# Sliding-window attention and a gated feed-forward block: where the attention ends, a fifth block by seven products, and sums on GpSimd

## The chip, the cores and the metric

The kernel runs on one core of one Trainium2 chip. A core has TensorE (PE, matrix products), VectorE (DVE) and ScalarE (ACT), which take TensorE's results out of PSUM, GpSimd (POOL), which can't reach PSUM and here issues the loads, and SyncE (SP), which issues stores and transposing transfers. The metric is the device time of one execution in microseconds, the median of several runs. A profile is of one execution of its own.

## The reference

```
attention, for each of 8 batches and 8 heads, 576 rows of 64:
scores = q k^T / 8, minus slope_h * distance, only where 0 <= distance < 128
attn = softmax(scores) v
x = attn as 4608 rows of 512 (8 heads of 64 side by side)
g = x w_gate          (512 -> 1536)
h = silu(g) * (x w_val)
out = h w_out         (1536 -> 512), float32
```

## The kernel before

**Attention.** The 4608 rows are cut into 36 tiles of 128, counted i = 0 to 35: two batches give nine tiles, the ninth of which joins the two last 64 rows. For each tile there are loads of q, k and v (from the POOL queue, seven tiles ahead, `loads_to`), transposed copies of q and k (`kT` has 12 places, `qT` 9), score products, an Exp on ScalarE, a multiplication with a mask on VectorE (lines 303 and 335), the products with v (line 359), a reciprocal and a multiplication (lines 362 and 363), and a transfer that writes the tile transposed into `xT` (line 381).

**Feed-forward.** Nine blocks n of 512 rows; block 8 collects the joined tiles, so it needs the last tile. A block has 12 slices m of 128 hidden columns. *Directly*, a slice is a product pg with the gate weights and one pv with the value weights, four matmuls of 512 columns each (line 415). pg and pv turn through three PSUM buffers. The gate is x*sigmoid(x), here made of Tanh on ScalarE (line 433), which shares its table with Exp, one VectorE instruction on pg (uu, line 434) and one on pv (hT, line 445); hT is twice the value, and the projection halves it.

*By seven products* (Strassen's scheme in Winograd's form), two slices make a unit u: seven products of four matmuls of 256 columns (line 639) stand for eight. They need sums of the weights (`gate_val_weight_sums`, four subtractions a unit of 128x512 f16) and of x (`x_sums`, four a block). Their gate is ScalarE's Silu, which needs another table, so it can only begin when the last Exp is done. `SEVEN_FROM = 6`: blocks 6, 7 and 8 go so.

**Projection.** From block 1 on the second product goes by seven products too (`strassen`, line 550): 14 parts a block of six matmuls of 256 columns, interleaved with the next block's first products. They need sums of h (`sums`, lines 503 to 506, in three chunks c of four instructions), which are put into a list, `later`, and issued one or two a step.

**Order.** The feed-forward generator yields steps: 1.0 for a direct product, 0.75 for a part of the projection, 0.5 for a product by seven. `everything` advances the attention to a target: from step 60 on, 84 + (step - 57) * RATE / 34.5 attention steps (line 1016); a direct block has 34.5 steps. TensorE's order is then as written; DVE and ACT are ordered by the scheduler, which may run an instruction earlier than it is written; POOL's and SP's queues keep the written order. In block 5, behind slice `SILU_AT = 7`, `attention_ends` runs what is left of the attention and brings in the Silu table (line 979); slices 8 to 11 then use Silu directly (lines 431 and 442). The weight sums and the sums of x go into `later` on VectorE (lines 613 to 616). Their results lie in places of kT, qT and the masks that the attention no longer needs (`t_homes`, `spare`).

Of the kernel before, what the change touches and what calls it, by code (L numbers as in the profile page):

```python
# [11 lines left out]
FP16 = mybir.dt.float16  # L12
# [17 lines left out]
FIRST = 4  # L30
LEAD = 6
PRE = 0
SEVEN_FROM = 6
SILU_AT = 7
SECOND = 5.5
RATE = 54.0
FIXED_FROM = 60
LATE = 13


def slot(h):
# [11 lines left out]
def kernel(  # L53
# [366 lines left out]
        return ps  # L420

    acted = {}
    by_silu = set()

    def gate(n, m, pg, c0=0, c1=512):

        if (n, m) not in acted:
            acted[(n, m)] = [supool.tile([P, 512], FP16, name=i, tag=i) for i in ("tt", "uu")]
        tt, uu = (t_[:, c0:c1] for t_ in acted[(n, m)])
        if (n, m) in by_silu:  # L430
            nc.scalar.activation(tt, pg[:, c0:c1], AF.Silu)
            return
        nc.scalar.activation(tt, pg[:, c0:c1], AF.Tanh, scale=0.5)  # L433
        nc.vector.scalar_tensor_tensor(out=uu, in0=tt, scalar=one if (n, m) == PIN else 1.0,  # L434
                                       in1=pg[:, c0:c1], op0=ALU.add, op1=ALU.mult)

    def val(n, m, pv, c0=0, c1=512):

        if n not in hT:
            hT[n] = hpool.tile([P, NMB, 512], FP16, name="hT", tag="hT")  # L440
        if (n, m) in by_silu:
            nc.vector.scalar_tensor_tensor(out=hT[n][:, m, c0:c1], in0=acted[(n, m)][0][:, c0:c1], scalar=2.0,
                                           in1=pv[:, c0:c1], op0=ALU.mult, op1=ALU.mult)
            return
        nc.vector.tensor_mul(hT[n][:, m, c0:c1], acted[(n, m)][1][:, c0:c1], pv[:, c0:c1])  # L445
# [52 lines left out]
    one_more = []  # L498
    hsum = {}

    def four_sums(a11, a12, a21, a22, s2, s3, s4):

        return [lambda: nc.vector.tensor_sub(s3, a11, a21),
                lambda: nc.vector.tensor_add(a21, a21, a22),
                lambda: nc.vector.tensor_sub(s2, a21, a11),
                lambda: nc.vector.tensor_sub(s4, a12, s2)]

    def at_once(fs):
        for f in fs:
            f()  # L510

    def sums(n, c):
# [7 lines left out]
        return four_sums(a11, a12, a21, a22, s2, s3, s4)  # L520

    def strassen(n, t):

# [3 lines left out]
        S2, S3, S4 = hsum[n]  # L527
        cols = slice(t * P, (t + 1) * P)
        end = n == NBLK - 1
        seeded = SEVEN_FROM <= n + 1 < NBLK  # L530
        factor = 1.0 if n >= SEVEN_FROM else 0.5
        if end:
            X, Y = (ps_a.tile([P, HC], FP32, name="po", tag="a", bufs=4) for _ in range(2))
# [73 lines left out]
    t_homes = [halves(kT[:, n]) for n in range(NK)] + [halves(qT[:, n]) for n in range(NQ)] + spare[6:9]  # L607

    def gate_val_weight_sums(u):

        cols = slice(2 * u * P, (2 * u + 2) * P)
        t1, t2, t3, t4 = tsum[u] = t_homes[4 * u:4 * u + 4]
        return [lambda: nc.vector.tensor_sub(t1, V1[:, :, cols], G1[:, :, cols]),
                lambda: nc.vector.tensor_sub(t3, V2[:, :, cols], V1[:, :, cols]),
                lambda: nc.vector.tensor_sub(t2, V2[:, :, cols], t1),
                lambda: nc.vector.tensor_sub(t4, G2[:, :, cols], t2)]

    def x_sums(n):

        a11, a12 = xT[n][:, 0:HK, 0:256], xT[n][:, HK:NKB, 0:256]  # L620
        a21, a22 = xT[n][:, 0:HK, 256:512], xT[n][:, HK:NKB, 256:512]
        s2, s3, s4 = xsum[n] = spare[3 * (n % 2):3 * (n % 2) + 3]
        return four_sums(a11, a12, a21, a22, s2, s3, s4)

    later = []

    def gate_val_by_seven(n):

        x = xT[n]
        A11, A12 = x[:, 0:HK, 0:256], x[:, HK:NKB, 0:256]  # L630
        S1, A22 = x[:, 0:HK, 256:512], x[:, HK:NKB, 256:512]
        S2, S3, S4 = xsum.pop(n)
        hT[n] = hpool.tile([P, NMB, 512], FP16, name="hT", tag="hT")
        live = {}

        def product(dst, w, c0, a, start=False):
# [59 lines left out]

    def seven_steps():

        units = [(n, u) for n in range(SEVEN_FROM, NBLK) for u in range(NMB // 2)]
        of = {}  # L700
        for i, (n, u) in enumerate(units):
            if u == 0:
                of[n] = gate_val_by_seven(n)
            now, before = (n, u), units[i - 1] if i else None
            if i + 1 < len(units):
                turn = (("first", now), ("seventh", before), ("fifth", now), ("sixth", now),
                        ("fourth", before), ("second", now), ("third", now))
            else:
                turn = (("first", now), ("seventh", before), ("fifth", now), ("sixth", now),
                        ("fourth", before), ("second", now), ("seventh", now), ("third", now),  # L710
                        ("fourth", now))
            for k, (name, which) in enumerate(turn):
                if which is not None:
                    of[which[0]][name](which[1])
                yield n, 7 * u + k, name, which
# [3 lines left out]
    def ffn():  # L719

        for n in range(NBLK):
            if n > 1:
                parts = chain(strassen(n - 1, 0), strassen(n - 1, 1))
            if n == 1:
                begin(2, 2, 1)
                begin(3, 3, 1)
                for j in range(PRE):
                    for _ in project(0, j, ps_f, "po", 1):
                        yield 1.0
            if n == SEVEN_FROM:  # L730
                break
            due, given = 0, 0
            for m in range(NMB):
                for half, _ in enumerate(gate_val(n, m)):
                    scored[0] = False
                    yield 1.0
                    due += n > 1 and 2 * m + half in AT
                    while due and not (scored[0] and given % 7 == 1):
                        next(parts)
                        due, given = due - 1, given + 1  # L740
                        yield 0.75
                    if n > 1:
                        for _ in range(1 + (len(later) > 3)):
                            if later:
                                later.pop(0)()
                if n == 1:
                    if m in (4, 6, 8, 10):
                        for _ in project(0, m // 2 - 2, ps_f, "po", 1):
                            yield 1.0
                    if m in (4, 6, 8):  # L750
                        weight_sums(m // 2 - 2)
                if n > 0 and m >= 9:
                    (at_once if n == 1 and m < 11 else later.extend)(sums(n, m - 9))
                if n + 1 == SEVEN_FROM:
                    if m == SILU_AT:
                        attention_ends()
                        by_silu.update((n, i) for i in range(m + 1, NMB))
                    if m in (SILU_AT + 1, SILU_AT + 2):
                        later.extend(gate_val_weight_sums(m - SILU_AT - 1))
                    if m == SILU_AT:  # L760
                        later.extend(x_sums(n + 1))
            if n > 1:
                assert next(parts, 0) == 0
        ends = [strassen(NBLK - 1, t) for t in range(2)]
        tail = ExitStack()
        for n, k, name, which in seven_steps():
            if k == 0 and n > SEVEN_FROM:
                assert next(parts, 0) == 0
                parts = chain(strassen(n - 1, 0), strassen(n - 1, 1))
            if n == SEVEN_FROM and k in (1, 3, 10, 17):  # L770
                later.extend(gate_val_weight_sums(2 + (k + 4) // 7))
            yield 0.5
            if k % 3 == 2 and k < 42:
                next(parts)
                yield 0.75
            if k == 20 and n + 1 < NBLK:
                later.extend(x_sums(n + 1))
# [97 lines left out]
    def attention():  # L875
# [5 lines left out]
        for i in range(FIRST, last + 1):  # L881
# [10 lines left out]
            if not late or i == last:  # L892
                weighted(i)
                yield i
            loads_to(i + 7)
            ahead(i)
            yield i - len(waiting)
            if late and i < X_DMA_FROM:
# [155 lines left out]
```

## Time and profile before

| what | us |
|---|---|
| median of 3 runs | 334.12 (333.97 to 334.51) |
| the profiled execution: time | 334.78 |
| the profiled execution: span | 333.0 |
| TensorE busy | 324.5 |
| VectorE busy | 273.4 |
| ScalarE busy | 202.5 |
| GpSimd busy (issuing loads) | 111.1 |
| last v products of the attention begin | 222 |
| first product by seven (line 639) begins | 236.61 |

The time is some 1.8 us longer than the span, which counts from the program's first to its last instruction. The page's slices are 8.3 us each, and a digit is the busy share in tenths. The ends of matmuls are modelled, so the cost of a product is better read from one start to the next. In the timeline, the first two numbers of a line are start and length in us, and `x4` counts the instructions merged into it.

### The profile page before, as it was taken

What the parts mean: (1) busy time and instruction counts of PE and PEld (TensorE: products, weight loads), DVE (VectorE), ACT (ScalarE), POOL (GpSimd) and SP (SyncE); (2) the same over time, 40 slices, a digit from 0 to 9 for tenths busy, and PEclk for the clock granted to TensorE, in tenths of its full rate; (3) what the DMA queues carried; (4) which work ended last, traced back from release to release, by engine and by line L of the source; (5) the groups of instructions that cost most, each with busy time, mean ns of one, the idle gap of its engine ahead of it and who ended that gap; (6) DMA issues with size and microseconds to landing.
All of it is one profiled execution on the core that took longest, in us unless ns stands there. A gap on an engine that the chain in (4) does not pass through costs nothing.

```text
span 333.0 us, 7659 instructions
## 1 busy us (share of the span) xinstructions
PE 324.5 (97%) x2919; PEld 216.6 (65%) x2919; DVE 273.4 (82%) x643; ACT 202.5 (61%) x404; POOL 111.1 (33%) x138
## 2 busy tenths in 40 slices
PE   8999999999999999999999999999999999999994
PEld 4575465544455655556555665666788888888884
DVE  3579878999798889987999999999854985775683
ACT  4885777465665656457456365563567666776650
POOL 8977776468853254553535000000000000000000
PEclk9999999999999999999999999999999999999999
DMA  9999999999999999999999664231100101011014
GB/s 151 171 182 175 174 186 166 119 131 182 178 173 142 189 159 150 165 151 185 197 132 164 136 81 111 18 94 19 65 31 33 63 2 66 25 42 63 2 63 128
DMA packets 166565, 38.82 MB, mean 117 GB/s; under 512 B 154368, under 2 KB 162176, under 8 KB 166528
## 3 DMA queue, kind: packets, MB, share of 16 engines
q0 software_dynamic: 118880, 18.62, 80.9%
q1 hardware_dynamic: 46960, 19.08, 30.5%
q10 hardware_dynamic: 688, 0.62, 0.6%
q8 instruction: 23, 0.38, 0.5%
q14 instruction: 14, 0.11, 0.1%
HBM read 37.91 MB, written 9.44 MB: 142 GB/s over the span
## 4 chain that ended last, share of the span: by engine, by line
PE 85%; DVE 10%; ACT 2%; issue 1%; DVEq 0%
PE po L550 18%; PE pg L415 16%; PE pv L415 15%; PE gX L639 9%; PE gY L639 5%; PE av L359 5%; PE ps L291 3%; PE p L550 3%; DVE uu L434 2%; PE gZ L639 2%; DVE hT L445 2%; PE psc L327 2%; PE po L469 2%; DVE ex L303 1%; ACT tt L433 1%
## 5 line engine op out<-in xcount | busy, mean ns | idle before, releaser
L415 PE MATMUL pv<-xT,wv_sb 128*128 128x512 f16 (+2 forms) x312 | 76.6, 363 | 0.3 <-DVE uu L434 0.2
L415 PE MATMUL pg<-xT,wg_sb 128*128 128x512 f16 (+2 forms) x324 | 76.5, 355 | 0.1
L433 ACT ACTIVATE tt<-pg 128x512 f16<-128x512 f32 x68 | 40.9, 603 | 48.9 <-PE pg L415 48.9
L297 ACT ACTIVATE ex<-ps 128x512 f16<-128x512 f32 x96 | 50.1, 607 | 8.0 <-PE ps L291 8.0
L434 DVE SCALAR_TENSOR_TENSOR uu<-tt,pg 128x512 f16<-128x512 f16 x67 | 45.6, 680 | 7.7 <-ACT tt L433 7.4
L190 POOL DMA_DIRECT2D kn<-in_k_dram x39 | 33.2, 854 | 43.9 <-DMA kT<-kn 31.4
L445 DVE TENSOR_TENSOR hT<-uu,pv 128x512 f16<-128x512 f16 x68 | 46.1, 679 | 1.6
L415 PEld LDWEIGHTS <-wg_sb 128*128 128x128 f16 x324 | 28.7, 98 | 24.0 <-issue 2.2
L550 PEld LDWEIGHTS <-hT 128*128 128x128 f16 x384 | 37.1, 98 | 10.7 <-issue 0.8
L415 PEld LDWEIGHTS <-wv_sb 128*128 128x128 f16 x312 | 27.9, 98 | 24.8 <-issue 2.3
L184 POOL DMA_DIRECT2D va<-in_v_dram x40 | 34.4, 866 | 15.5 <-DMA kT<-kn 6.6
L190 POOL DMA_DIRECT2D qn<-in_q_dram x39 | 33.3, 863 | 8.7 <-DMA qT<-qn 3.2
L550 PEld LDWEIGHTS <-S 128*128 128x128 f16 x288 | 27.5, 98 | 8.0 <-issue 1.5
L303 DVE TENSOR_TENSOR ex<-ex,m_reg 128x1024 f16<-128x1024 f16 x42 | 28.5, 684 | 2.8 <-ACT ex L297 2.8
L363 DVE TENSOR_TENSOR x<-av,rec 128x256 f16<-128x256 f32 x72 | 28.4, 419 | 0.5
L550 PE MATMUL po<-T,S 128*128 128x256 f16 x192 | 25.9, 273 | 0.3 <-ACT u2s L576 0.3
L550 PE MATMUL po<-T,hT 128*128 128x256 f16 x192 | 26.0, 273 | 0.0
L331 ACT ACTIVATE exc<-psc 128x512 f16<-128x512 f32 x40 | 21.4, 608 | 3.2 <-PE psc L327 3.1
L693 DVE TENSOR_TENSOR hT<-s,v 128x512 f16<-128x512 f16 x18 | 7.6, 424 | 17.7 <-ACT s L692 17.7
L359 PEld LDWEIGHTS <-ex 128*128 128x128 f16 x384 | 17.5, 98 | 4.4 <-issue 1.0
L359 PE MATMUL av<-va,ex 128*128 128x65 f16 x384 | 19.3, 193 | 0.3 <-ACT ex L297 0.3
L291 PE MATMUL ps<-qT,kT 64*128 64x256 f16 x192 | 15.9, 272 | 1.4 <-DVE qT L222 0.6
(129 smaller groups left out, 522.3 us busy)
## 6 DMA issues: line engine op xcount, KB each, us to landing
out_dram<-osb SPq DMA_DIRECT2D x32, 256.0 KB, 2.2
va<-in_v_dram POOLq DMA_DIRECT2D x32, 128.0 KB, 6.2
qn<-in_q_dram POOLq DMA_DIRECT2D x31, 128.0 KB, 6.6
kn<-in_k_dram POOLq DMA_DIRECT2D x31, 128.0 KB, 6.2
wg_sb<-in_moe_w_gate_dram POOLq DMA_DIRECT2D x6, 256.0 KB, 7.6
wo_sb<-in_moe_w_out_dram POOLq DMA_DIRECT2D x3, 512.0 KB, 8.4
wv_sb<-in_moe_w_val_dram POOLq DMA_DIRECT2D x5, 256.0 KB, 7.6
kn<-in_k_dram POOLq DMA_DIRECT2D x8, 64.0 KB, 4.7
```

The source lines that it names most:

```text
L184: nc.gpsimd.dma_start(va[rank][p0:p1, :, 0:D], src)
L190: nc.gpsimd.dma_start(t_[p0:p1], src)
L297: nc.scalar.activation(e[:, o:o + 2, :], banks[q4][par], AF.Exp, scale=scale)
L303: nc.vector.tensor_mul(e[:, o, :], e[:, o, :], reg[:, o, :])
L359: nc.tensor.matmul(av[:, j, :], w, val, start=(n == 0), stop=(n == len(todo) - 1))
L363: nc.vector.tensor_mul(x[:, 4 * half:4 * half + 4, :], av[:, :, 0:D], rec.broadcast_to([P, 4, D]))
L415: nc.tensor.matmul(ps[:, c0:c1], w[:, kb, ms], xT[n][:, kb, c0:c1], start=(kb == 0 and c0 == 0), stop=(kb == NKB - 1 and c1 == 512), skip_ ...
L433: nc.scalar.activation(tt, pg[:, c0:c1], AF.Tanh, scale=0.5)
L434: nc.vector.scalar_tensor_tensor(out=uu, in0=tt, scalar=one if (n, m) == PIN else 1.0, in1=pg[:, c0:c1], op0=ALU.add, op1=ALU.mult)
L445: nc.vector.tensor_mul(hT[n][:, m, c0:c1], acted[(n, m)][1][:, c0:c1], pv[:, c0:c1])
L550: nc.tensor.matmul(dst, a[:, m, cols], b[:, m, :], start=(start and m == 0), stop=(m == HM - 1), skip_group_check=True)
L639: nc.tensor.matmul(dst[:, i, :], w[:, kb, c0 + i * P:c0 + (i + 1) * P], a[:, kb, :], start=(start and i == 0 and kb == 0), stop=(i == 1 an ...
```

## The change

- Block 5 goes by seven products from slice 4 on (`SEVEN_FROM = 5`, `UNIT_FROM = 2`: its units 2 to 5). Slices 0 to 3 stay direct, with Tanh; their hT is halved on the spot (the factor 0.5 in line 438's function), since a block by seven holds h itself. The direct Silu slices are gone.
- `attention_ends` stands behind slice 3 of block 5, and RATE is 59.
- All weight sums run on GpSimd: those of the first three units used (u = 2, 3, 4) are issued at attention tiles 29, 30 and 33, the other three behind the attention's end. The sums of x of block 5 run on GpSimd at tile 31, with a place of their own for s1, as the direct slices still read x. The first chunk of the h sums of blocks 3 and 4 runs on GpSimd, behind slice 10.
- The places of all these sums are chosen anew, by when the attention frees them. In `strassen` the second product of block 4's first half keeps its old buffers, and block 4's projection runs on among the units of block 5.

```diff
-SEVEN_FROM = 6
-SILU_AT = 7
+SEVEN_FROM = 5
+UNIT_FROM = 2
 SECOND = 5.5
-RATE = 54.0
+RATE = 59.0
...
+SUMS_BY_POOL = {3, 4}
...
-        if (n, m) in by_silu:
-            nc.vector.scalar_tensor_tensor(out=hT[n][:, m, c0:c1], in0=acted[(n, m)][0][:, c0:c1], scalar=2.0,
+        if n == SEVEN_FROM:
+            nc.vector.scalar_tensor_tensor(out=hT[n][:, m, c0:c1], in0=acted[(n, m)][1][:, c0:c1], scalar=0.5,
                                            in1=pv[:, c0:c1], op0=ALU.mult, op1=ALU.mult)
...
-        seeded = SEVEN_FROM <= n + 1 < NBLK
+        seeded = SEVEN_FROM <= n + 1 < NBLK and (n >= SEVEN_FROM or t > 0 or UNIT_FROM == 0)
...
+    turns = [(UNIT_FROM + n) % (NMB // 2) for n in range(NMB // 2)]
+    t_homes = dict(zip(turns, (early_homes[0:4], early_homes[4:8], early_homes[12:16],
+                               late_homes[0:4], late_homes[4:8], late_homes[8:12])))
...
-        return [lambda: nc.vector.tensor_sub(t1, V1[:, :, cols], G1[:, :, cols]),
-                lambda: nc.vector.tensor_sub(t3, V2[:, :, cols], V1[:, :, cols]),
-                lambda: nc.vector.tensor_sub(t2, V2[:, :, cols], t1),
-                lambda: nc.vector.tensor_sub(t4, G2[:, :, cols], t2)]
+        t1, t2, t3, t4 = tsum[u] = t_homes[u]
+        return [lambda: nc.gpsimd.tensor_sub(t1, V1[:, :, cols], G1[:, :, cols]),
+                lambda: nc.gpsimd.tensor_sub(t3, V2[:, :, cols], V1[:, :, cols]),
+                lambda: nc.gpsimd.tensor_sub(t2, V2[:, :, cols], t1),
+                lambda: nc.gpsimd.tensor_sub(t4, G2[:, :, cols], t2)]
...
-            for m in range(NMB):
+            for m in range(2 * UNIT_FROM if n == SEVEN_FROM else NMB):
...
-                if n > 0 and m >= 9:
+                if n > 0 and m >= 9 and (m > 9 or n not in SUMS_BY_POOL):
                     (at_once if n == 1 and m < 11 else later.extend)(sums(n, m - 9))
...
+                if m == 10 and n in SUMS_BY_POOL:
+                    at_once(sums(n, 0, nc.gpsimd))
+            if n == SEVEN_FROM:
+                break
...
+        attention_ends()
+        for u in turns[3:]:
+            at_once(gate_val_weight_sums(u))
...
+            if i in (29, 30):
+                at_once(gate_val_weight_sums(turns[i - 29]))
+            if i == 31:
+                at_once(x_sums(SEVEN_FROM))
+            if i == 33:
+                at_once(gate_val_weight_sums(turns[2]))
```

More of the change, by code (lines that the diff above doesn't have):

```diff
@@ L422 @@
     acted = {}
-    by_silu = set()
     def gate(n, m, pg, c0=0, c1=512):
@@ L429, in gate @@
         tt, uu = (t_[:, c0:c1] for t_ in acted[(n, m)])
-        if (n, m) in by_silu:
-            nc.scalar.activation(tt, pg[:, c0:c1], AF.Silu)
-            return
         nc.scalar.activation(tt, pg[:, c0:c1], AF.Tanh, scale=0.5)
@@ L440, in val @@
             hT[n] = hpool.tile([P, NMB, 512], FP16, name="hT", tag="hT")
-        if (n, m) in by_silu:
-            nc.vector.scalar_tensor_tensor(out=hT[n][:, m, c0:c1], in0=acted[(n, m)][0][:, c0:c1], scalar=2.0,
+        if n == SEVEN_FROM:
+            nc.vector.scalar_tensor_tensor(out=hT[n][:, m, c0:c1], in0=acted[(n, m)][1][:, c0:c1], scalar=0.5,
                                            in1=pv[:, c0:c1], op0=ALU.mult, op1=ALU.mult)
@@ L499, with four_sums @@
     hsum = {}
[L501 to L506, printed above, removed]
+    def four_sums(a11, a12, a21, a22, s2, s3, s4, s1=None, eng=nc.vector):
+        s1 = a21 if s1 is None else s1
+        return [lambda: eng.tensor_sub(s3, a11, a21),
+                lambda: eng.tensor_add(s1, a21, a22),
+                lambda: eng.tensor_sub(s2, s1, a11),
+                lambda: eng.tensor_sub(s4, a12, s2)]
     def at_once(fs):
@@ L510, in at_once, with sums @@
             f()
-    def sums(n, c):
+    def sums(n, c, eng=nc.vector):
         if n not in hsum:
@@ L519, in sums @@
         s2, s3, s4 = (t_[:, lo, :] for t_ in hsum[n])
-        return four_sums(a11, a12, a21, a22, s2, s3, s4)
+        return four_sums(a11, a12, a21, a22, s2, s3, s4, eng=eng)
     def strassen(n, t):
@@ L606 @@
     spare += [halves(m_[:, 4 * n:4 * n + 4, :]) for m_ in msk for n in range(2)]
-    t_homes = [halves(kT[:, n]) for n in range(NK)] + [halves(qT[:, n]) for n in range(NQ)] + spare[6:9]
+    early_homes = [halves(t_[:, n]) for t_, n in ((kT, 0), (kT, 1), (kT, 2), (kT, 3), (qT, 0), (kT, 4),
+                                                  (qT, 1), (kT, 5), (qT, 2), (qT, 3), (kT, 7), (qT, 4),
+                                                  (kT, 8), (qT, 5), (kT, 9), (qT, 6))]
+    late_homes = [halves(t_[:, n]) for t_, n in ((kT, 6), (kT, 10), (kT, 11), (qT, 7), (qT, 8))] + spare[3:10]
+    turns = [(UNIT_FROM + n) % (NMB // 2) for n in range(NMB // 2)]
+    t_homes = dict(zip(turns, (early_homes[0:4], early_homes[4:8], early_homes[12:16],
+                               late_homes[0:4], late_homes[4:8], late_homes[8:12])))
+    x_homes = {SEVEN_FROM: early_homes[8:11] + early_homes[11:12]}
+    for n in range(SEVEN_FROM + 1, NBLK):
+        x_homes[n] = early_homes[8:11] if (n - SEVEN_FROM) % 2 == 0 else spare[0:3]
     def gate_val_weight_sums(u):
         cols = slice(2 * u * P, (2 * u + 2) * P)
-        t1, t2, t3, t4 = tsum[u] = t_homes[4 * u:4 * u + 4]
-        return [lambda: nc.vector.tensor_sub(t1, V1[:, :, cols], G1[:, :, cols]),
-                lambda: nc.vector.tensor_sub(t3, V2[:, :, cols], V1[:, :, cols]),
-                lambda: nc.vector.tensor_sub(t2, V2[:, :, cols], t1),
-                lambda: nc.vector.tensor_sub(t4, G2[:, :, cols], t2)]
+        t1, t2, t3, t4 = tsum[u] = t_homes[u]
[3 more added lines that the diff above has]
+                lambda: nc.gpsimd.tensor_sub(t4, G2[:, :, cols], t2)]
     def x_sums(n):
@@ L621, in x_sums @@
         a21, a22 = xT[n][:, 0:HK, 256:512], xT[n][:, HK:NKB, 256:512]
-        s2, s3, s4 = xsum[n] = spare[3 * (n % 2):3 * (n % 2) + 3]
-        return four_sums(a11, a12, a21, a22, s2, s3, s4)
+        s2, s3, s4 = x_homes[n][0:3]
+        s1 = x_homes[n][3] if n == SEVEN_FROM else a21
+        xsum[n] = s1, s2, s3, s4
+        return four_sums(a11, a12, a21, a22, s2, s3, s4, s1, nc.gpsimd if n == SEVEN_FROM else nc.vector)
     later = []
@@ L630, in gate_val_by_seven @@
         A11, A12 = x[:, 0:HK, 0:256], x[:, HK:NKB, 0:256]
-        S1, A22 = x[:, 0:HK, 256:512], x[:, HK:NKB, 256:512]
-        S2, S3, S4 = xsum.pop(n)
-        hT[n] = hpool.tile([P, NMB, 512], FP16, name="hT", tag="hT")
+        A22 = x[:, HK:NKB, 256:512]
+        S1, S2, S3, S4 = xsum.pop(n)
+        if n not in hT:
+            hT[n] = hpool.tile([P, NMB, 512], FP16, name="hT", tag="hT")
         live = {}
@@ L697, in seven_steps @@
     def seven_steps():
-        units = [(n, u) for n in range(SEVEN_FROM, NBLK) for u in range(NMB // 2)]
+        units = [(n, u) for n in range(SEVEN_FROM, NBLK)
+                 for u in range(UNIT_FROM if n == SEVEN_FROM else 0, NMB // 2)]
         of = {}
         for i, (n, u) in enumerate(units):
-            if u == 0:
+            if n not in of:
                 of[n] = gate_val_by_seven(n)
@@ L729, in ffn @@
                         yield 1.0
-            if n == SEVEN_FROM:
+            due, given = 0, 0
+            if n == SEVEN_FROM and not UNIT_FROM:
                 break
-            due, given = 0, 0
-            for m in range(NMB):
+            for m in range(2 * UNIT_FROM if n == SEVEN_FROM else NMB):
                 for half, _ in enumerate(gate_val(n, m)):
@@ L751, in ffn @@
                         weight_sums(m // 2 - 2)
-                if n > 0 and m >= 9:
+                if n > 0 and m >= 9 and (m > 9 or n not in SUMS_BY_POOL):
                     (at_once if n == 1 and m < 11 else later.extend)(sums(n, m - 9))
[L754 to L761, printed above, removed]
+                if m == 10 and n in SUMS_BY_POOL:
+                    at_once(sums(n, 0, nc.gpsimd))
+            if n == SEVEN_FROM:
+                break
             if n > 1:
                 assert next(parts, 0) == 0
+        attention_ends()
+        for u in turns[3:]:
+            at_once(gate_val_weight_sums(u))
         ends = [strassen(NBLK - 1, t) for t in range(2)]
@@ L769, in ffn @@
                 parts = chain(strassen(n - 1, 0), strassen(n - 1, 1))
-            if n == SEVEN_FROM and k in (1, 3, 10, 17):
-                later.extend(gate_val_weight_sums(2 + (k + 4) // 7))
             yield 0.5
-            if k % 3 == 2 and k < 42:
-                next(parts)
+            if k % 3 == 2 and k < 42 and next(parts, 1) is None:
                 yield 0.75
```

## The prediction

> **What bounds the kernel now.** I read the page from the top: busy shares first, then the slices, then the chain of waits, then sums of busy time by stage.
>
> ```profile
> PE 324.5 (97%) x2919; PEld 216.6 (65%) x2919; DVE 273.4 (82%) x643; ACT 202.5 (61%) x404; POOL 111.1 (33%) x138
> ...
> PE   8999999999999999999999999999999999999994
> ...
> DVE  3579878999798889987999999999854985775683
> ...
> POOL 8977776468853254553535000000000000000000
> ...
> PE 85%; DVE 10%; ACT 2%; issue 1%; DVEq 0%
> ```
>
> TensorE is busy nearly everywhere and carries 85% of the chain that ended last. VectorE is the only other engine with a share there. It stands at 9 in slices 18 to 26, which is the last third of the attention. GpSimd does nothing after slice 21. The sums by stage (us, then busy PE, PEld, DVE, ACT, POOL) sharpen this:
>
> ```profile
> 150.00:190.00 40.00, 39.93 (x374) 24.20 (x373) 38.15 (x92) 23.03 (x47) 15.13 (x19) 1.00 1.70 165
> 190.00:222.00 32.00, 32.00 (x298) 19.12 (x297) 31.58 (x79) 19.64 (x40) 0.00 (x0) 1.00 0.40 71
> 222.00:236.60 14.60, 14.56 (x103) 8.75 (x100) 14.53 (x40) 5.02 (x11) 0.00 (x0) 1.00 0.23 55
> 236.60:264.10 27.50, 27.50 (x253) 24.65 (x252) 18.05 (x40) 19.00 (x38) 0.00 (x0) 1.00 0.10 40
> ```
>
> From 190 to 222 us both TensorE and VectorE have no idle time. From 236.6 us on, the blocks by seven products, VectorE is free a third of the time. So there are two questions: how many TensorE microseconds go, and what happens to a VectorE that has nothing to spare. How near it stands to TensorE's need is seen in the timeline around the end of the attention (start, length, engine):
>
> ```profile
> 218.20 1.02 PE L415 MATMUL pg<-xT,wg_sb 128*128 128x512 f16 x4
> 219.06 1.03 PE L415 MATMUL pv<-xT,wv_sb 128*128 128x512 f16 x4
> 220.74 1.03 PE L415 MATMUL pg<-xT,wg_sb 128*128 128x512 f16 x4
> 221.43 0.68 DVE L434 SCALAR_TENSOR_TENSOR uu<-tt,pg 128x512 f16<-128x512 f16 x1
> 222.33 1.02 PE L415 MATMUL pv<-xT,wv_sb 128*128 128x512 f16 x4
> ```
>
> pg and pv turn through three PSUM buffers, so the pv at 222.33 takes the buffer of the pg at 218.20. VectorE frees that at 221.43 + 0.68 = 222.11, which is 0.22 us before TensorE wants it.
>
> **TensorE: the products.** From the same lines a direct product (four matmuls of 512 columns) costs 219.06 - 218.20 = 0.86 us from start to start. Two slices m are four products, 3.45 us. A unit by seven does the same work in seven products of four matmuls of 256 columns:
>
> ```profile
> 241.63 0.60 PE L639 MATMUL gY<-xT,kT 128*128 128x256 f16 x4
> 242.06 0.60 PE L639 MATMUL gX<-m_reg,kT 128*128 128x256 f16 x4
> 242.50 0.60 PE L639 MATMUL gX<-xT,kT 128*128 128x256 f16 x4
> 242.94 0.82 PE L550 MATMUL po<-T,S 128*128 128x256 f16 x6
> ```
>
> That is (242.94 - 241.63)/3 = 0.437 us each, 3.06 us a unit. A unit saves 0.39 us. Slices 4 to 11 of block 5 become four units: 4 x 0.39 = **1.6 us less**, all of it on the path, since TensorE sets it. Nothing else on TensorE changes in number: the second projection's products and the attention are the same matmuls, elsewhere.
>
> **ScalarE.** Eight activations (8 x 0.60) become four units of two Silu and three copies (20 x 0.59): 7.0 us more within about 18 us. The full blocks by seven already run so, with ScalarE at 19.0 of 27.5 us and TensorE without idle time, so this is hidden at 0. The table load (1.28 us at 219.88) now comes just ahead of the first unit, not four slices ahead of it. At present TensorE does not stop over it. The first unit's sixth product waits for a ScalarE copy of the first; if that copy stands behind the load, I bound the wait by 0 and 1.28 us and take 0.3, since a fifth product (0.44) and a part of the projection (0.65) lie between.
>
> **VectorE: what goes.** Its instructions overlap at the ends: the timeline steps 0.60 us behind one of 0.68 and 0.33 behind one of 0.41. The 24 weight sums are 24 x 0.33 = 8 us, and they are not run behind the attention, where the program puts most of them: 14 of the 24 start before 222 us (lines 613 to 616, from 150.1 us on), and 3 sums of x too. In 190 to 222 that is 4 + 3 sums, 2.3 us. Four h sums of block 4 go as well, 1.3 us. Against it the attention is pressed together: 283 attention steps end at step 57 + (283-84) x 34.5/54 = 184 of the ffn count now, and at 57 + (283-84) x 34.5/59 = 173 with RATE 59. Block 5 begins at 163.5 and its four direct slices end at 175, so nothing is left over to be run in a heap. Per ffn step the attention rises by 9%, TensorE's time by some 2%: VectorE's attention work in this stretch (masks 6.8, x and rec 6.2 us) grows by about 0.8 us. Sum: 0.4 idle + 2.3 + 1.3 - 0.8 = **3.2 us of air in 32**. By itself this buys no time, since the waits of 190 to 222 us name none of TensorE; earlier, in the five 20 us windows from 60 to 160 us, TensorE's busy time lacks 1.2 us in all. I bound the gain by 0 and that 1.2 us and take 0.2.
>
> **GpSimd: what comes.** 24 weight sums, 4 sums of x, 8 of h: 36 instructions on two SBUF inputs of 128x512 f16. The trace has none on this engine. From below one costs what VectorE needs, 0.33 us; from above the longest instruction of any compute engine but TensorE, the 1.28 us table load. I take 0.87, GpSimd's only row of work (issuing a load, 0.85 to 0.87 us). All loads are issued by 181 us, so only the h sums of block 3 have loads behind them (rank 33 on); in the trace that rank's v load waits until 171.76 us anyway. Behind that, twelve sums are queued at tiles 29 to 31; tile 29 comes at step 143, block 4's h sums at 158, and a step takes about 1 us (a block's 34.5 steps span 36 us), so they have 15 us: at 0.87 they take 10.4, at 1.28 15.4. The h sums are due at the third part of the next projection, 9 steps after their place. So GpSimd's own lateness costs 0 at either end.
>
> The open price is what GpSimd does to VectorE. Before the first unit 20 of these instructions run in about 32 us. From below each costs VectorE nothing; from above each holds it for its whole length, 20 x 0.87 = 17 us. VectorE's instructions with two SBUF inputs in 190 to 222 (masks, h sums, fillers) are about a third of its busy time, so I take a third of half the length, 20 x 0.14 = 2.9 us, just inside the 3.2 us of air: cost 0.3 us.
>
> The Trainium skill ("SBUF — State Buffer", section "Who interferes with whom") speaks against this change: a VectorE instruction with two SBUF inputs contends with a GpSimd one that reads SBUF, and the later one waits for the whole of the other. The trace shows no such pair. The skill's "GPSIMD Engine Reference", section 3.1, gives about 2.6 cycles of 1.2 GHz an element for two inputs, an estimate of 1.1 us here; by these two pages some 15 of the 20 would hold VectorE for half of that, 8 us, and the sum would be about 2.5 us slower instead of faster.
>
> **Sum.** -1.6 + 0.3 (switch) - 0.2 + 0.3 = **-1.2 us**. The span of 333.0 becomes 331.8. The profiled execution took 334.78, 0.66 above the median of the runs, so I put the difference on the median: 334.12 - 1.2 = **332.9 us**.
>
> **Rivals.**
> 1. *VectorE held by GpSimd* (slower). Place: tiles 29 to 35, before the first unit. Each of 20 GpSimd sums meets a mask or an h sum and holds it for half its length: 20 x 0.44 = 8.7 us, less 3.2 us of air and about 1 us of buffers, 4.5 us of TensorE waiting for PSUM: 334.1 - 1.6 + 4.5 = 337.0. It decides from a hold of 0.25 us per instruction on ((3.2 + 1.6)/20). For it: 0.22 us between uu and pv. Against it: two thirds of VectorE's time is on PSUM or single inputs, and its air is real. A half-sized hold gives 335.
> 2. *GpSimd late* (slower): at 2.0 us an instruction the twelve take 24 us, block 4's h sums start 9 us late, and the first two of them end 13 us after their place against 9: 4 us of stop, 332.9 + 4 = 336.9. It decides from 1.7 us an instruction (12 x 1.7 - 15 + 2 x 1.7 = 8.8).
> 3. *Given back*: the 1.6 us goes to the switch of tables and to attention latencies, since the masks and AV of a tile have 9% less other work between them (TensorE's busy time falls to 19.44 of 20 us between 120 and 140 us, beside masks): within 0.2%, 333.5 to 334.8.
> 4. *Air pays*: an unfilled VectorE ends earlier before each AV, and the 1.2 us that TensorE lacks between 60 and 160 us goes: 332.9 - 1.2 = 331.7.
>
> **How the numbers follow.** Forecast 0.45 (332.2 to 333.4), rival 4 0.08, rival 3 0.13, rival 1 0.27, rival 2 0.07. Faster by over 0.2% (0.67 us, about what a measurement here can tell from no change): 0.53. Same: 0.13. Slower: 0.34. The range runs from just under rival 4's 331.7 to just past rival 1's 337.0, and leaves out the far end of the holding price and a gain above 2.5 us.
>
> **What would show it.** Right: the four units of block 5 at 0.437 us a product; the first unit (L639) starting near 217 us, 20 us sooner than now (the fifth direct slice now begins at 214.67, and some 2 us of TensorE's attention work behind it moves ahead); VectorE below 95% in the 32 us ahead of it; no weight sums on it. Wrong: masks, h sums or products of two SBUF inputs on VectorE that last longer than 0.68 and 0.42 us while GpSimd works, pv matmuls waiting for uu, L550 waiting for a GpSimd sum, or a GpSimd sum above 1.3 us.

## The result and the profile after

The changed kernel takes **347.52 us** (median of 4 runs, 345.02 to 348.12) beside 334.19 us before. The ratio is 1.038 with an interval of 1.0355 to 1.0413: 13 us slower, where 1.2 us faster was forecast. The profiled execution took 347.09 us, its span 345.3. Times are medians, and the two executions that ran in a slower state (663.12 us in run 1, 351.50 us in run 11) are left out of them.

First the page of the changed kernel: busy times, four rows of the 40 slices, and the shares of the chain of waits.

```profile
PE 325.5 (94%) x2967; PEld 221.8 (64%) x2967; DVE 277.9 (80%) x615; ACT 209.4 (61%) x416; POOL 156.2 (45%) x174
...
PE   8999999999999999999988994979999999999994
...
DVE  4778978999797799888998989885885785785582
...
POOL 8977774639835274366849766690000000000000
PEclk9999999999999999999999998799999999999999
...
PE 63%; DVE 20%; DMA 8%; issue 4%; ACT 3%; ACTq 0%; DVEq 0%
```

TensorE's share of the chain fell from 85 to 63%, VectorE's doubled from 10 to 20%, and DMA, which had none, has 8%. TensorE's row has a hole at slice 25, and just there the granted clock, which stood at 9 in every slice before, drops. From block 6 on nothing differs: 96.4 us to the end of the span in both (236.6 to 333.0 before, 248.9 to 345.3 after). Block 4 starts 2.0 us later than before, block 5 6.2 us, and block 6 12.3 us. So most of the loss lies in blocks 4 and 5, where 32 of the 36 GpSimd sums run.

The sums by stage (start:end, us, then busy PE, PEld, DVE, ACT, POOL, the granted TensorE clock as a share of full speed, DMA share, GB/s), first of the kernel before:

```profile
200.00:210.00 10.00, 10.00 (x86) 5.84 (x86) 10.00 (x28) 5.38 (x12) 0.00 (x0) 1.00 0.34 93
210.00:220.00 10.00, 10.00 (x101) 6.03 (x102) 10.00 (x24) 6.27 (x14) 0.00 (x0) 1.00 0.26 28
```

then of the changed kernel, around the hole:

```profile
200.00:210.00 10.00, 9.25 (x92) 5.52 (x91) 9.39 (x16) 5.79 (x12) 8.67 (x7) 1.00 0.04 9
210.00:220.00 10.00, 5.81 (x31) 2.72 (x31) 9.13 (x16) 2.45 (x5) 4.50 (x5) 0.66 0.37 86
220.00:230.00 10.00, 8.70 (x88) 5.79 (x87) 10.00 (x20) 4.39 (x8) 9.84 (x9) 1.00 0.13 26
```

In the changed kernel VectorE is busy for 9.13 to 10 of every 10 us, but with 16 to 20 instructions, where 24 to 28 filled such a 10 us before. A busy share that stays while the count falls means longer instructions. VectorE's timeline in front of the hole (start, length):

```profile
207.77 1.64 DVE L336 TENSOR_TENSOR exc<-exc,m_reg 128x1024 f16<-128x1024 f16 x1
209.33 1.37 DVE L503 TENSOR_TENSOR S<-hT 128x512 f16<-128x512 f16 x1
210.62 1.37 DVE L501 TENSOR_TENSOR S<-hT 128x512 f16<-128x512 f16 x1
211.91 1.63 DVE L336 TENSOR_TENSOR exc<-exc,m_c 128x1024 f16<-128x1024 f16 x1
213.46 0.67 DVE L431 SCALAR_TENSOR_TENSOR uu<-tt,pg 128x512 f16<-128x512 f16 x1
```

and GpSimd's, for the same stretch:

```profile
206.23 1.34 POOL L620 TENSOR_TENSOR kT<-wv_sb,wg_sb 128x512 f16<-128x512 f16 x1
207.53 1.33 POOL L621 TENSOR_TENSOR kT<-wv_sb 128x512 f16<-128x512 f16 x1
208.82 1.59 POOL L622 TENSOR_TENSOR qT<-wv_sb,kT 128x512 f16<-128x512 f16 x1
210.49 1.21 POOL L623 TENSOR_TENSOR qT<-wg_sb,qT 128x512 f16<-128x512 f16 x1
211.66 1.33 POOL L620 TENSOR_TENSOR kT<-wv_sb,wg_sb 128x512 f16<-128x512 f16 x1
```

Laid side by side they take strict turns. GpSimd's sum ends at 207.53 + 1.33 = 208.86, and the mask ends 0.55 us later, at 209.41. GpSimd's next sum is listed from 208.82, but it ends 1.00 us after that mask, at 210.41; VectorE's sum ends 0.29 us behind it. By these ends it looks as if neither engine worked while the other did. The four VectorE instructions take 5.7 us from start to start (207.77 to 213.46); by the steps that the prediction read (0.60 a mask, 0.33 a sum) they need 1.9. The `uu` at 213.46 was queued behind them, and it frees the PSUM buffer of a `pg`. TensorE's timeline:

```profile
208.23 1.03 PE L416 MATMUL pg<-xT,wg_sb 128*128 128x512 f16 x4
214.19 1.87 PE L416 MATMUL pv<-xT,wv_sb 128*128 128x512 f16 x4 [4.93 <-DVE uu L431]
215.85 1.49 PE L548 MATMUL po<-wo_sb,hT 128*128 128x256 f16 x6
217.27 1.04 PE L328 MATMUL psc<-qT,kT 64*128 64x128 f16 x16
218.23 1.72 PE L416 MATMUL pg<-xT,wg_sb 128*128 128x512 f16 x4
219.79 1.03 PE L416 MATMUL pv<-xT,wv_sb 128*128 128x512 f16 x4
```

The stop of 4.93 us is the hole. The four groups behind it run at about half rate: 1.66, 1.42, 0.96 and 1.56 us from start to start, where undisturbed ones take 0.86, 0.65, 0.55 and 0.86. That is 2.7 us more. The clock in the row of 210 to 220 us is 0.66 because it is half of full speed for part of it:

```profile
212.80:219.60 6.80, 5.41 (x30) 2.59 (x30) 5.93 (x14) 2.08 (x5) 1.38 (x3) 0.50 0.27 51
```

VectorE's groups over the whole kernel, by shape (count, then busy us and mean ns), the changed kernel's first:

```profile
L304 DVE TENSOR_TENSOR ex<-ex,m_reg 128x1024 f16<-128x1024 f16 x42 | 31.1, 747 | 4.6 <-ACT ex L298 4.4
L501 DVE TENSOR_TENSOR S<-hT 128x512 f16<-128x512 f16 x22 | 11.8, 545 | 0.0
L336 DVE TENSOR_TENSOR exc<-exc,m_c 128x1024 f16<-128x1024 f16 x12 | 10.5, 879 | 4.5 <-ACT exc L332 4.3
L336 DVE TENSOR_TENSOR exc<-exc,m_reg 128x1024 f16<-128x1024 f16 x7 | 7.5, 1073 | 1.8 <-ACT exc L332 1.8
```

and one of the kernel before:

```profile
L303 DVE TENSOR_TENSOR ex<-ex,m_reg 128x1024 f16<-128x1024 f16 x42 | 28.5, 684 | 2.8 <-ACT ex L297 2.8
```

Before, every mask group had a mean of 683 to 686 ns and every group of h sums 414 to 418. Only instructions that read two SBUF tiles (masks, sums of h and of x) grew; `uu` and `hT`, which read PSUM, kept 0.68 us. Counted one by one, 19 VectorE instructions were lengthened, by 13.9 us together (0.73 each). GpSimd's 36 sums take 46.0 us, mean 1.28; those that meet nothing take 1.15.

**A ledger on TensorE** of the two profiled executions. New waits: pv for uu 5.7 - 0.2 = 5.5; the output projection for `osb` (VectorE's copy out of PSUM) 2.3; scores for q's transposing transfer 1.5 + 1.1 = 2.6. Half clock 2.7. Units -1.6. Sum +11.5, of 347.09 - 334.78 = 12.3. The rest is not assigned.

### The profile page after: what moved, and what is told of

The parts are those of the page before. It is cut to its first block, busy times and chain, and to the rows that moved or that the text cites. A ratio compares the mean times of both kernels' runs of the same rounds, so it can differ in the third digit from the quotient of the medians.

```text
span 345.3 us, 7787 instructions
## 1 busy us (share of the span) xinstructions
PE 325.5 (94%) x2967; PEld 221.8 (64%) x2967; DVE 277.9 (80%) x615; ACT 209.4 (61%) x416; POOL 156.2 (45%) x174
## 4 chain that ended last, share of the span: by engine, by line
PE 63%; DVE 20%; DMA 8%; issue 4%; ACT 3%; ACTq 0%; DVEq 0%
PE po L548 14%; PE gX L649 11%; PE pv L416 9%; PE pg L416 8%; DMA qT<-qn 7%; PE gY L649 5%; DVE uu L431 4%; DVE hT L442 3%; PE gZ L649 3%; PE av L360 3%; PE p L548 2%; DVE exc L336 2%; DVE ex L304 2%; PE ps L292 2%; DVE x L364 2%
## 5 line engine op out<-in xcount | busy, mean ns | idle before, releaser
L416 PE MATMUL pv<-xT,wv_sb 128*128 128x512 f16 (+2 forms) x280 | 69.2, 365 | 5.9 <-DVE uu L431 5.7
L416 PE MATMUL pg<-xT,wg_sb 128*128 128x512 f16 (+3 forms) x292 | 69.0, 356 | 0.5 <-DVE hT L442 0.4
L430 ACT ACTIVATE tt<-pg 128x512 f16<-128x512 f32 x64 | 38.6, 604 | 41.9 <-PE pg L416 41.8
L431 DVE SCALAR_TENSOR_TENSOR uu<-tt,pg 128x512 f16<-128x512 f16 x63 | 42.8, 680 | 6.9 <-ACT tt L430 6.6
L416 PEld LDWEIGHTS <-wv_sb 128*128 128x128 f16 x280 | 25.1, 98 | 29.2 <-issue 10.4
L442 DVE TENSOR_TENSOR hT<-uu,pv 128x512 f16<-128x512 f16 x60 | 40.7, 680 | 1.8 <-PE pv L416 0.3
L416 PEld LDWEIGHTS <-wg_sb 128*128 128x128 f16 x292 | 25.7, 98 | 22.5 <-issue 3.2
L304 DVE TENSOR_TENSOR ex<-ex,m_reg 128x1024 f16<-128x1024 f16 x42 | 31.1, 747 | 4.6 <-ACT ex L298 4.4
L703 DVE TENSOR_TENSOR hT<-s,v 128x512 f16<-128x512 f16 x22 | 9.3, 425 | 19.8 <-ACT s L702 19.8
L664 ACT COPY p<-gY 128x512 f32<-128x512 f32 x22 | 12.9, 585 | 12.2 <-PE gY L649 11.8
```

Source lines behind the costliest of these rows:

```text
L304: nc.vector.tensor_mul(e[:, o, :], e[:, o, :], reg[:, o, :])
L416: nc.tensor.matmul(ps[:, c0:c1], w[:, kb, ms], xT[n][:, kb, c0:c1], start=(kb == 0 and c0 == 0), stop=(kb == NKB - 1 and c1 == 512), skip_ ...
```

## The experiments

Theory 1: GpSimd's sums hold VectorE because both read SBUF, each instruction waiting for the other's whole length. Theory 2: the units, the denser attention or the table switch cost the time. Theory 3, formed on the way: the pressed attention also outruns its transfers.

**1. All 36 sums back on VectorE** (everything else as in the changed kernel).

```
-        return [lambda: nc.gpsimd.tensor_sub(t1, ...
+        return [lambda: nc.vector.tensor_sub(t1, ...
...
-                    at_once(sums(n, 0, nc.gpsimd))
+                    at_once(sums(n, 0))
```

> The changed kernel with all 36 sums back on VectorE, everything else as changed. Theory 1 (GpSimd's sums hold VectorE's two-input instructions): masks back at 0.68 us and sums at 0.42, the 5 us stop of TensorE at 209 us gone; VectorE has some 12 us of sums more, so 333 to 337 us. Theory 2 (the attention is pressed too hard, whoever makes the sums): still 344 us or more, since VectorE gets more to do.

Measured 336.9 us (six executions, 335.67 to 338.08), ratio 1.007 (1.004 to 1.0099). No lengthened instruction: masks 0.685. 10.6 of the 13.3 us are gone, as theory 1 said, at the upper end of its range. 2.7 us above the kernel before are left, so something else costs too (runs 3, 6 and 8).

**2. Only the weight sums of the kernel before on GpSimd** (24 sums, no other edit: `nc.vector` to `nc.gpsimd` in the same four lines).

> The kernel before with its 24 weight sums on GpSimd, nothing else. Theory 1: masks and h sums beside them are held by up to 1 us each, 24 GpSimd sums of 1.2 us; VectorE loses 8 us of its own sums and gains up to 15 us of holding: 335 to 341 us. Theory 2: 333 to 334.5 us, as VectorE is relieved.

342.40 us, ratio 1.0244 (1.0208 to 1.028). With no unit, no RATE and no switch touched, 24 sums (31.5 us on GpSimd) cost 8.2 us; 13 VectorE instructions are lengthened, by 8.4. pv waits 2.7 us for uu. The cost exceeds what was expected, as did that of the change.

**3. Only RATE 54 to 59 in the kernel before.**

> The kernel before with RATE 59 alone: the attention runs 9% faster against the feed-forward, nothing else moves. Theory 1: 333.5 to 335.5 us, the attention ends some 8 us sooner. Theory 2: 338 us or more, with TensorE waiting for masks and for loads.

335.55 us, ratio 1.0046 (1.0015 to 1.0076): just above theory 1's range and far below theory 2's. TensorE's timeline of this run shows what the pressed attention meets:

```profile
174.06 0.61 PE L291 MATMUL ps<-qT,kT 64*128 64x256 f16 x8 [1.21 <-DMA qT<-qn]
```

The scores of a tile now come before q's transposing transfer has landed. The kernel before has no such wait.

**4. The changed kernel with fills in the place of GpSimd's sums** (same places and tiles; nothing is read, so no fill waits for an input).

```
-        return [lambda: nc.gpsimd.tensor_sub(t1, V1[:, :, cols], G1[:, :, cols]),
+        return [lambda: nc.gpsimd.memset(t1, 0.0),
...
```

> The changed kernel, each GpSimd sum replaced by a fill of the same output (128x512 f16): the values are left out, GpSimd writes SBUF at the same places and reads nothing. Theory 1 in its narrow form (the shared thing is GpSimd's reading): no held mask, 332 to 335 us. In its wide form (any GpSimd work holds VectorE): masks above 1 us still, 338 or more. Theory 2: 344 or more.

334.54 us, ratio 1.0013 (0.9976 to 1.0051); its ten executions spread from 333.45 to 338.08, so this median is sure to about 1.3 us either way. 13.0 us go by taking GpSimd's reading (and, with it, more than half of each instruction's length) away. VectorE's timeline of this run at the same place in the program:

```profile
204.16 0.69 DVE L336 TENSOR_TENSOR exc<-exc,m_reg 128x1024 f16<-128x1024 f16 x1
204.76 0.42 DVE L505 TENSOR_TENSOR S<-hT 128x512 f16<-128x512 f16 x1
205.09 0.42 DVE L503 TENSOR_TENSOR S<-hT 128x512 f16<-128x512 f16 x1
205.43 0.69 DVE L336 TENSOR_TENSOR exc<-exc,m_c 128x1024 f16<-128x1024 f16 x1
```

GpSimd's timeline has a fill that ends within the first of them:

```profile
203.99 0.52 POOL L622 MEMSET kT<- 128x512 f16 x1
```

and among VectorE's groups of the whole run the masks of ex read:

```profile
L304 DVE TENSOR_TENSOR ex<-ex,m_reg 128x1024 f16<-128x1024 f16 x42 | 28.6, 686 | 7.7 <-ACT ex L298 7.5
```

These are the same four instructions as at 207.77 above: 1.9 us instead of 5.7. The mask at 204.16 runs beside the fill until 204.51 and keeps its length, and over all 42 masks the mean is 686 ns, as before. Scores still wait 2.6 us for q's transfers.

**5. Copies in the place of GpSimd's sums** (one SBUF input each; the values of the sums are left out).

```
+            return [lambda to=to, of=of: eng.tensor_copy(to, of)
+                    for to, of in ((s3, a11), (s1, a22), (s2, s1), (s4, s2))]
...
```

> The changed kernel, each GpSimd sum replaced by a copy of one of its inputs (the sums' values are left out): GpSimd reads one SBUF input, not two, and the instruction is shorter. If any GpSimd reading holds VectorE's two-input instructions, masks beside them lie between 0.8 and 1.2 us, and the time is between the fills' 334.5 and the sums' 347.5 us, by the length of a copy: 337 to 342. If only the reading of two inputs does it, masks stay at 0.69 us and the time at 333.5 to 335.5.

338.49 us, ratio 1.0139 (1.0087 to 1.0192). A copy alone takes 0.61 us, near a fill's 0.52, yet 12 VectorE instructions are lengthened, by 4.4 us: most held masks take 1.09, one 1.57. VectorE's timeline of this run has

```profile
212.96 1.09 DVE L336 TENSOR_TENSOR exc<-exc,m_c 128x1024 f16<-128x1024 f16 x1
```

and GpSimd's, at the same time,

```profile
212.71 0.80 POOL L623 COPY qT<-wv_sb 128x512 f16<-128x512 f16 x1
```

The mask ends 0.54 us behind the copy, as masks did 0.55 us behind a sum. So a single read on GpSimd is enough to hold VectorE; the shorter instruction holds for less (0.40 us here, 0.95 at 207.77), and the kernel loses less.

**6. Fills, and transfers one tile earlier** (run 4 with AHEAD 4 to 5).

> The changed kernel with fills in place of GpSimd's sums (their values are left out) and the transfers of q and k one tile sooner: no holding, no stop for transfers. If the 1.6 us of TensorE reach the end, 332.5 to 333.3 us, 0.3 to 0.5% faster than before. If something else in the earlier end of the attention takes them back, 333.8 to 335.

332.87 us, ratio 0.9957 (0.9941 to 0.9974): 0.4% faster than the kernel before, clear of the noise. The waits for q's transfers are gone, worth 334.54 - 332.87 = 1.7 us, to within run 4's spread. This is what the change would be if its sums were free. The stage that held the trouble, 190 to 220 us, in this run:

```profile
190.00:220.00 30.00, 29.24 (x282) 19.10 (x281) 26.14 (x64) 17.76 (x36) 9.47 (x20) 1.00 0.39 79
```

VectorE is at 26.14 of 30 us, 87%; and the first unit starts at 215.9 us.

**7. The kernel before with RATE 59 and AHEAD 5.**

> The kernel before with RATE 59, and the transposing transfers of q and k issued one tile sooner (AHEAD 5). The pressed kernel alone took 0.46% more than before, with TensorE's stops of 0.9 and 1.4 us at scores that wait for q's transfer at 117 and 174 us. If these transfers are the price of pressing, both stops go: 333.6 to 334.6 us. If it is VectorE or ScalarE, still 335 to 336.

334.07 us, ratio 0.9998 (0.9979 to 1.0018): with the earlier transfers the price of run 3 is gone, and no price of attention latency is left that these runs can tell from nothing. The stops at 117 and 174 us are gone; in the profiled execution (334.75 us) a stop of 1.09 us for q's transfer stands at 189.53 instead.

**8. All sums on VectorE with AHEAD 5.**

> The changed kernel, all sums on VectorE, transfers one tile sooner. What is left against the fills is VectorE's own 12 us of sums in a stretch that is full: 335.3 to 337.0 us. If stops for transfers were all that VectorE's version lost, 332.5 to 333.5.

335.61 us, ratio 1.0046 (1.0029 to 1.0063). What stays are waits for VectorE (osb 1.9 us, exc 0.9). In 190 to 220 us of run 1 VectorE was busy 29.86 of 30: with the sums at home it has no air, and the 332.87 of run 6 is not reached.

**9. No h sums on GpSimd** (`SUMS_BY_POOL = set()`, 28 sums stay there).

> The changed kernel with the eight h sums of blocks 3 and 4 back on VectorE; weight sums and x sums stay on GpSimd. If each GpSimd sum costs in proportion, 28 of 36 are left: 343.5 to 346. If the loss comes of a few sums that stand just ahead of the units (weight sums of tile 33 and behind the attention's end), nearly unchanged: 346 to 348.5.

343.40 us, ratio 1.027 (1.0231 to 1.0309). 16 lengthened, 9.4 us. Eight sums fewer save 4.1 us, more than their share of the 13.0 us (2.9). So the loss is not that of a few sums just ahead of the units.

**10. Each GpSimd sum in two halves** (128x256 each).

```
+        def in_two(out, one, two):
+            for k_ in range(2):
+                nc.gpsimd.tensor_sub(out[:, k_], one[:, k_], two[:, k_])
...
```

> The changed kernel, each GpSimd sum cut in two of 128x256, same values. If VectorE is held to the end of the GpSimd instruction that is running, a hold is half as long (masks near 1.1 instead of 1.6 us) and half of the 13 us of the sums is gone: 339 to 343. If it is held as long as GpSimd has work queued, or by a share of its bandwidth, nothing is won: 346 to 349, as 72 instructions take longer in sum than 36.

353.52 us, ratio 1.0586 (1.0548 to 1.0624): worse than either figure. A hold by one half is indeed half as long (a mask beside halves takes 1.15 us, a half 0.66), but VectorE's timeline has this:

```profile
188.66 9.06 DVE L304 TENSOR_TENSOR ex<-ex,m_reg 128x1024 f16<-128x1024 f16 x2
```

and GpSimd's, in the meantime:

```profile
189.03 1.29 POOL L631 TENSOR_TENSOR kT<-wv_sb,qT 128x256 f16<-128x256 f16 x2
190.29 1.29 POOL L631 TENSOR_TENSOR kT<-wg_sb,kT 128x256 f16<-128x256 f16 x2
191.54 2.53 POOL L504 TENSOR_TENSOR qT<-xT 128x256 f16<-128x256 f16 x4
194.04 1.28 POOL L504 TENSOR_TENSOR qT<-qT,xT 128x256 f16<-128x256 f16 x2
195.29 1.28 POOL L504 TENSOR_TENSOR kT<-xT,qT 128x256 f16<-128x256 f16 x2
```

Twelve halves run without a gap while a mask waits and a second stands behind it; the first takes 8.46 us, a lengthening of 7.8. So a waiting VectorE instruction does not always get the next turn: GpSimd instructions queued back to back can pass it. The changed kernel has one such case too (a mask of 2.43 us that starts at 183.13, beside a sum listed from 182.68, and ends at 185.56, 0.55 us behind the end of the next sum).

**11. A short fill behind each GpSimd sum**, to give VectorE a turn (`nc.gpsimd.memset(turn, 0.0)` on one column).

> The changed kernel with a fill of one column behind each GpSimd sum. In the kernel with halved sums one pair of masks was passed over by GpSimd instructions for 8 us. If VectorE gets its turn whenever GpSimd runs an instruction that reads nothing, no hold is longer than one sum (1.2 us; masks at most 1.9 us) and the time falls to 342 to 346. If not, 347 to 350, as GpSimd has 36 instructions more.

345.40 us (three executions, 345.39 to 347.33), ratio 1.0348 (1.0315 to 1.0381): inside the first range, but its executions overlap with the changed kernel's (345.02 to 348.12), so a gain is not shown. No lengthening exceeds 0.96 us now, where the changed kernel had 1.75, but 19 of them still add 12.7 us and the 5 us stop stays. So passing over is a small part of the loss, and the ordinary holds are the large one.

**12. Only the 12 weight sums put behind the attention on GpSimd**, the other 24 sums on VectorE.

```
...
-            at_once(gate_val_weight_sums(u))
+            at_once(gate_val_weight_sums(u, nc.gpsimd))
```

> The changed kernel with only the twelve weight sums behind the attention's end on GpSimd; the other 24 sums on VectorE. Behind the end VectorE has few instructions with two SBUF inputs and a third of its time free. If holding costs only where VectorE is full, these twelve relieve it: 335.5 to 337.5, at or under the 337.7 of all sums on VectorE. If a GpSimd sum costs the same wherever it stands (13 us / 36 = 0.36 us each), 339 to 342.

340.73 us, ratio 1.0206 (1.0173 to 1.0238): in the second range. But the run does not test what it was made for. The expectation had these sums behind the attention's end, beside the units, where VectorE has room. GpSimd's timeline of this run (the bracket: idle time before, and what ended it):

```profile
202.00 1.26 POOL L620 TENSOR_TENSOR kT<-wv_sb,wg_sb 128x512 f16<-128x512 f16 x1 [21.30 <-PE psc L328]
208.14 1.37 POOL L621 TENSOR_TENSOR kT<-wv_sb 128x512 f16<-128x512 f16 x1 [4.88 <-PE psc L328]
209.47 1.34 POOL L622 TENSOR_TENSOR kT<-wv_sb,kT 128x512 f16<-128x512 f16 x1
```

They stand late in the program, but GpSimd's queue is empty by then, and each starts as soon as the scores that last read its tile are done: from 202 us on, beside the last masks, and all twelve ahead of the first unit at 224.2. 8 VectorE instructions are lengthened by 5.2 us, pv waits 2.6 for uu and a product with v 2.2 for a mask. What a sum beside the units would cost stays open.

**13 to 15. Two units instead of four** (UNIT_FROM 4, RATE 54), which leaves room for a mended version: with all sums on VectorE, with the 12 late ones on GpSimd, and with all on VectorE, RATE 59 and AHEAD 5.

> The changed kernel with all sums on VectorE, the attention's end behind slice 7 of block 5 as before, RATE 54, and two units of block 5 by seven (8 direct slices). Two units save 0.8 us of TensorE, the attention isn't pressed, and VectorE has four sums of x more and the weight sums at written places: 333.2 to 335.0 us. If the switch to the units behind the table load has a price of its own, 335 to 337.

> Attention's end behind slice 7 of block 5, RATE 54, two units of block 5 by seven, the twelve late weight sums on GpSimd, the rest on VectorE. With all on VectorE this took 335.1. If GpSimd is harmless behind the attention: 333.5 to 335.2; if not, 336 to 338.5.

> Attention's last place behind slice 7 of block 5, RATE 59 (it ends some four slices sooner), transfers one tile sooner, two units by seven, all sums on VectorE, which finds air for them in the four slices between. 0.8 us of TensorE less: 333.2 to 334.3 us if VectorE's fullness was what stopped the version with RATE 54 (335.1); else 335 to 336.

335.14 us (1.0025, 1.001 to 1.0039), 340.07 (1.0163, 1.0139 to 1.0188) and 334.38 (1.001, 0.9997 to 1.0023). The first and third lie slightly above what was expected. The second lies 1.6 us above its higher range; as in run 12, all its GpSimd sums run ahead of the first unit, and 8 instructions are lengthened by 4.6 us. No version with its real sums beats the kernel before.

## Why the prediction was wrong

By the runs' medians the +13.4 us (347.52 against the 334.13 that the kernel before took beside run 6) divide into three: **-1.3** for what the change would bring with free sums and earlier transfers (run 6 against before), **+1.7** for q's transfers (run 4 against run 6), **+13.0** for GpSimd reading SBUF (the changed kernel against run 4; the stops and the half clock behind them included). Run 4's spread leaves the cut between the last two loose by about 1.3 us.

- **The units: right.** From 231.82 to 232.25 and from 234.87 to 235.31 and 235.75 a product costs 0.435 us (0.437 said). -1.6 was said for this term and -1.2 for the whole; without the two troubles the runs give -1.3. That this is so near the forecast is in part luck, since run 6 has fills and earlier transfers, which the forecast had not.
- **The first unit near 217 us:** at 228.2 in the changed kernel, at 215.9 in run 6.
- **The table switch, 0.3:** at the first unit TensorE does stop for 2.3 us, but for `osb` on VectorE (L553), a backlog, not for the table: the load ran at 220.67 us, 7.6 us ahead of the unit. No wait for the load is seen here or in run 6 (a stop of 0.76 us there, again for `osb`).
- **GpSimd late: rightly put at 0,** though a sum takes 1.15 us alone and 1.28 in the mean, not 0.87. No wait for a GpSimd sum is among TensorE's.
- **VectorE's air, 3.2 us of 32: about right.** Run 6 leaves 3.9 us of 30.
- **The failed step:** "so I take a third of half the length, 20 x 0.14 = 2.9 us, just inside the 3.2 us of air: cost 0.3 us." Each factor was too small. The length was 1.28 rather than 0.87. Not 20 but 33 of the 36 sums start ahead of the first unit (29 of them from 181 us on), as those that the program puts behind the attention don't wait for its end (run 12 shows why). The mean lengthening per sum is 13.9/36 = 0.39 us, not 0.14. VectorE's share of two-input instructions was taken as the chance of a hit, and at "about a third" it was low as well (14.7 of 37.4 us of instruction lengths in 190 to 222 us). The timeline at 207 us shows something else: while GpSimd has sums queued, each two-input instruction is held by the sum that runs, and the next one by the next sum. The air is an average over 32 us; the hits come in rows, 3.8 us within 5.7, and three PSUM buffers cover 0.2 us. Against run 4 the loss is near the sum of the lengthenings: 13.0 us for 13.9 here, 4.0 for 4.4 in run 5, 19.0 for 18.7 in run 10, and 10.9 for 12.7 in run 11.
- **Rival 1 had the mechanism, the place and the waiting matmul** (pv for uu) and was given 0.27. Its price of 8.7 us of holding was 13.9, and it lacked the 2.7 us at half clock. Its last figure does not follow from its own sum: a half-sized hold, 4.35 us, less 3.2 and 1 gives 332.7, not 335, under its own rule that it decides from 0.25 us on.
- **Rivals 3 and 4:** with nothing held and no late transfers, run 6 takes 332.87, between rival 4's 331.7 and rival 3's 333.5 to 334.8. Run 4 lies in rival 3's range, but for its transfers, which rival 3 did not name.
- **"Pressed by 9%"** was priced on VectorE alone and cost 1.5 us on transfers (run 3 against run 7).

The Trainium skill's rule that the prediction named ("SBUF — State Buffer", section "Who interferes with whom") was the better price: 8 us of holding and 2.5 us slower, still too little. The runs bear out both halves of it, that GpSimd's reads hold a two-input VectorE instruction (sums 0.73 a hit, copies 4.4 us in 12 hits) and that its writes alone don't (masks 0.686 beside fills). By its letter, though, the one that comes later waits for an instruction of the other; run 10's masks waited for a dozen.

**Open:** what decides between taking turns (207 to 213 us) and passing over (183 us, and run 10); and how the 13.0 us divide between the stops with their half clock and the many small delays, which no run separates.

## What to carry to other kernels

An engine with idle time is no free place for work if its reads hold up an engine that has no time to spare: price each moved instruction as a hold of its whole length on whatever it meets, and ask where hits in a row meet the shallowest buffer. Count a moved instruction where its queue lets it start, not where the program writes it. When a part of the program is pressed together, its loads have to be issued earlier by as much.

## What the runs showed of the hardware

- A GpSimd instruction on 128x512 f16 takes 1.15 us with two inputs, 0.61 as a copy and 0.52 as a fill; VectorE's two-input sum takes 0.41. Only the sums and the copies, which read SBUF, hold VectorE's two-input instructions.
- The holding goes both ways: GpSimd's own sums are stretched from 1.15 to 1.60 us by the masks that they meet.
- GpSimd instructions queued back to back can keep a VectorE instruction waiting for 7.8 us; a one-column fill between them kept every lengthening below 1 us.
- After a stop of 4.9 us TensorE's next four groups took nearly twice their time; the granted clock is 0.50 from 212.8 to 219.6 us, and 1.00 again from 219.6. After shorter stops it differs. One of 2.3 us (for osb, at 228.8 us) is followed by a full clock, 1.00 from 232 to 240 us. One of 2.4 us in run 11 (up to 229.8 us) is followed by 0.50 from 230.8 to 234.2, and with one of 2.2 us in run 2 (up to 223.65 us) the clock is 0.50 from 223.3 to 226.7. In run 12 two stops of 2.5 and 2.2 us within 6 us go with 0.92 and 0.90 in 210 to 220 and 220 to 230 us. What decides is not shown.
